# Scans of two prepared units moved behind later steps, and 21 products that nothing reads, in a fused RWKV-7 and hard-swish kernel

## The chip, the core and the metric

The kernel runs on one core of one Trainium2 chip. The metric is device time in microseconds (us) of one execution; the time of a version is the median of its runs. The core has a matrix engine (TensorE, PE in the profile, with the loads of its stationary operand shown apart as PEld), a vector engine (VectorE, DVE), a scalar engine (ScalarE, ACT), a general engine (GpSimd, POOL), and a queue that issues DMA transfers (SyncE, SP). Each takes its own instructions in program order; semaphores hold an instruction until what it needs is done.

## What is computed

The first half is the RWKV-7 recurrence over 4 batches, 8 heads, 768 steps and head size 40. The second is a feed-forward layer with hard-swish over the 3072 tokens, of width 320, with 2048 hidden features:

```python
for t in range(S):
    y[:, :, t] = einsum('bhd,bhde->bhe', rt, state)
    Sa = einsum('bhde,bhe->bhd', state, at)
    state = state * wt[:, :, None, :] - einsum('bhd,bhe->bhde', Sa, bt) \
            + einsum('bhd,bhe->bhde', vt, kt)
...
x = y.transpose(0, 2, 1, 3).reshape(B * S, H * D)
h = x @ w_in
out = (h * clip(h + 3.0, 0.0, 6.0) / 6.0) @ w_out
```

The two weight matrices arrive as 64-bit floats, which the kernel converts itself.

## The kernel before, in words

**Units.** Time is cut into blocks of 64 steps. A unit is one block of two of the four batches (128 rows) with all 8 heads; there are 24 units, and four consecutive ones (two blocks of both pairs of batches) make a group. Units 0 to 3 are the first group. For each unit the recurrence inside a block becomes dense algebra. `prepare` (line 532 on) makes what does not depend on the state: `W` turns the decays on PE (line 484) and multiplies them up with scans on DVE (lines 545, 549, 555); `gam` scans back and writes the decay factors (lines 564, 566, 568 and 579 on DVE, 583, 584 and 586 on POOL); then `A`, `B`, `K`, `F`, `E`, `EV` and `factor`. `step` (line 832) is the part that goes from unit to unit: `RT` and `VT` turn two inputs, `R`, `U` and `UT` solve for the block's updates with the inverse `tinv`, `C` and `H` are masked score products (line 522, masked on DVE at line 530), `sn` adds to the state (lines 961 and 969), `S` copies the turned state (lines 890 and 895), `rS` and `y` make the output, and `move` and `move2` bring it by 8 DMAs into the layout `xt` that the feed-forward part reads. A digit before a step is its unit: `2C` is the score product of unit 2.

**The inverse.** Each group needs the inverse of a triangular matrix for each head. `invert` (line 728) does the 32x32 parts on DVE in 30 dependent rounds of a product and a sum (lines 753 and 759) and ends with two transposes (lines 762 and 767). For the first group `third_block` then does the remaining blocks on PE, in two halves called `X` and `Y`: products at line 788, copied by ACT to `zs` (line 796), products at line 811, copied by ACT to `tinv` (line 821). The loop at line 1251 issues the rounds of the first inversion one instruction at a time; a counter `n` counts them, and at chosen values it slips in other work.

**Weights.** `load_weights` and `power` bring 20 pieces of the weights: a DMA (line 334), three ACT instructions (lines 384 to 386), and three DVE instructions (lines 369, 372, 360).

**Feed-forward.** `expand` (line 1060) makes hidden features on PE (line 1066), ACT and DVE apply the activation (lines 1081 and 1082, result `gt`), and `contract` (line 1099) multiplies by the second matrix (line 1107). `pieces` deals it out in small portions among the recurrence's work, so that PE always has something to do.

**Order around the change.** Nothing is scheduled automatically: the order in which Python issues is the order on each engine. Between the end of the first inversion and the steady loop the order is the table `PLAN` (line 1282), a row at a time. `P` and `Q` stand for units 4 and 5: the first mention runs the unit's `W`, the second its `gam`. `W` of unit 4 also issues two DMAs on SP that refill its input for unit 6. From row 8 on, counted from 0, feed-forward portions are dealt between the rows. The PSUM banks are shared: `one`, `o`, and buffers of two banks called `pair` and (until row 8) `lent`.

Of the kernel before, what the change touches and what calls it, by code (L numbers as in the profile page):

```python
# [17 lines left out]
P = 128  # L18
# [7 lines left out]
def _ap(ap, extra, dims):  # L26

    return bass.AP(tensor=ap.tensor, offset=ap.offset + extra, ap=[list(ap.ap[0])] + dims)
# [3 lines left out]
def kernel(  # L32
# [42 lines left out]
    nc = tc.nc  # L75
# [21 lines left out]
    def bank(tag, shape, bufs):  # L97
        return ps.tile(shape, F32, name=tag, tag=tag, bufs=bufs)
# [42 lines left out]
    def ps_pair(*dims):  # L141

        n = 1
        for d in dims:
            n *= d
        if shared[0] is None or shared[1] + n > 512:
            shared[:] = pair(), 0
            open_half[0] = None
        at = shared[1]
        shared[1] += n  # L150
        views, step = [], n
        for d in dims:
            step //= d
            views.append([step, d])
        t = shared[0][:]
        return [_ap(t, at, views), _ap(t, at + 512, views), _ap(t, at, [[512, 2]] + views)]
# [4 lines left out]
    ident = const.tile([P, P], F32, name="ident")  # L161
    nc.gpsimd.affine_select(
        out=ident[:], in_=ones, pattern=[[1, P]],
# [4 lines left out]
        out=ones[:, 0:BL], in_=ones[:, 0:BL], pattern=[[1, BL]],  # L168
# [3 lines left out]
        out=ones[BL:P, 0:BL], in_=ones[BL:P, BL:P], pattern=[[1, BL]],  # L172
# [7 lines left out]
    warm = const.tile([P, 1], F32, name="warm")  # L180
# [27 lines left out]
    start = const.tile([P, SCAN], F32, name="start")  # L208
# [167 lines left out]
    def power():  # L376

        to, raw = loaded[powered[0]]
        powered[0] += 1
        top = raw.rearrange("p n c t -> p n (c t)").bitcast(I16)[:, :, 3::4]  # L380
        if len(to.shape) == 4:
            top = top.rearrange("p n (j c) -> p n j c", c=to.shape[3])
        bits = to.bitcast(I32)
        nc.scalar.activation(out=bits, in_=top, func=AF.Identity, bias=low[:, 2:3], scale=1.0 / 16.0)
        nc.scalar.activation(out=to, in_=bits, func=AF.Prelu, bias=low[:, 0:1], scale=-1.0, alpha=2.0 ** -40)
        nc.scalar.activation(out=bits, in_=to, func=AF.Prelu, bias=low[:, 1:2], scale=-2.0 ** 63,
                             alpha=2.0 ** -40)
# [340 lines left out]
    def invert(F, third, alone=False):  # L728
# [46 lines left out]
            nc.gpsimd.tensor_copy(tinv[z + L:z + BL, :, L:BL], tb[z + L:z + BL])  # L775
        yield

    def third_block(F, tb, tt, n, zs, first=False):


        parts = [slice(0, H)]
        zp = ps_pair(H, L)
        for h in range(H):
            for y in range(2):
                for x in range(2):
                    z = x * BL
                    g = n * H + 2 * h + y
                    nc.tensor.matmul(out=zp[x][z + y * L:z + y * L + L, h, :], lhsT=F[z + L:z + BL, g, L:BL],
                                     rhs=tb[z + L:z + BL, g, :], start=True, stop=True,
                                     tile_position=(z + L, z + y * L))  # L790
        yield PE
        for part in parts:
            for x in range(2):
                z = x * BL
                for y in range(2):
                    nc.scalar.activation(out=zs[z:z + L, y, part], in_=zp[x][z + y * L:z + y * L + L, part],
                                         func=AF.Copy)
        if first:
            for part in parts:
                heads = slice(n * H + 2 * part.start, n * H + 2 * part.stop)  # L800
                for z in range(0, P, BL):
                    nc.gpsimd.tensor_copy(tinv[z:z + L, heads, 0:L], tb[z:z + L, heads])
                    nc.gpsimd.tensor_copy(tinv[z + L:z + BL, heads, L:BL], tb[z + L:z + BL, heads])
        shared[0] = None
        yield DONE
        tp = ps_pair(H, L)
        for h in range(H):
            for y in range(2):
                for x in range(2):
                    z = x * BL  # L810
                    nc.tensor.matmul(out=tp[x][z + y * L:z + y * L + L, h, :],  # L811
                                     lhsT=tt[z:z + L, n * H + 2 * h + y, :],
                                     rhs=zs[z:z + L, y, h, :], start=True, stop=True,
                                     tile_position=(z, z + y * L))
        yield PE
        for part in parts:
            for x in range(2):
                z = x * BL
                for y in range(2):
                    heads = slice(n * H + 2 * part.start + y, n * H + 2 * part.stop + y - 1, 2)  # L820
                    nc.scalar.activation(out=tinv[z:z + L, heads, L:BL],  # L821
                                         in_=tp[x][z + y * L:z + y * L + L, part], func=AF.Copy)
        shared[0] = None
        yield DONE


    def third_blocks(first=False):

        zs = inv.tile([P, 2, 2, H, L], F32, name="zs", tag="x", bufs=1)
        return [third_block(*third[-1], 2 * n, zs[:, n], first) for n in range(2)]  # L830
# [318 lines left out]
    def aside(n, weight=0):  # L1149

        for _ in range(n):
            if side and next(side[0], side) is side:
                side.popleft()
            due[0] += weight
            while due[0] >= 1:
                due[0] -= 1
                next(weights, None)
# [6 lines left out]
    def run(stage, steps=0, mixed=0, deals=0):  # L1164

        for at in stage:
            if at == DONE:
                return
            aside(steps, mixed)
            deal(deals)  # L1170
# [79 lines left out]
    n, cleared = 0, []  # L1250
    while not third:
        aside(1)
        if not third:
            n += 1
            if n in POWERS and powered[0] < len(loaded):
                power()
            if n in STEPS:
                next(weights, None)
            if converted[0] >= 2 and not cleared:
                cleared.append(True)  # L1260
                for z in range(0, P, BL):
                    nc.scalar.activation(out=tinv[z + L:z + BL, :, 0:L], func=AF.Copy, scale=0.0,
                                         in_=_ap(three[z + L:z + BL], 0, [[0, NH], [0, L]]))
            if n % EARLY == 0 and early:
                run(early.popleft())
# [6 lines left out]
    def block(i, j):  # L1272

        if i % NU < 2:
            if j == 0:
# [4 lines left out]


    PLAN = """X X:2 0U:4 0UT:2 1R
              0sn:2 0H:1 Y:2 P
              1U 1UT:2 0y P
              2RT:1 Y:1 Q
              1sn:1 1H:1 2VT:2 0move 0move2
              1y:2 2R Q
              2S:3 3RT:2
              1move 1move2 2U:2 2UT:1 2C:3
              3R:2 3VT  # L1290
              2rS:1 2sn:2 2H:2 3S:2
              2y:2 3U:1 3UT:1 3C:4
              3rS:1 3sn:2 3H:4 2move
              3y:3 2move2
# [193 lines left out]
```

## Time and profile before

| what | us |
|---|---|
| runs of the kernel | 790.04, 790.25 (median), 790.51 |
| the profiled execution: its own time | 791.42 |
| the profiled execution: its span | 789.70 |
| PE busy in the span | 729.7 |
| DVE busy | 496.0 |
| ACT busy | 320.6 |
| POOL busy | 174.7 |

The span reaches from the first to the last instruction of one profiled execution; 1.72 us lie around it. PE is busy for 92% of the span, but this is an average. From 300 to 500 us it is busy for 198.36 of 200 us; from 40 to 60 us for 4.87 of 20. All times in the text are from the span's start. PEclk is the share of the full TensorE clock that was granted: at 0.50 a product takes about twice as long.

### The profile page before, as it was taken

How to read it: one execution, taken by the hardware profiler on the slowest of the kernel's cores; microseconds unless marked ns; L12 is line 12 of the kernel's file. 1: busy time of each engine (PE TensorE's matmuls, PEld its weight loads, DVE VectorE, ACT ScalarE, POOL GpSimd, SP SyncE). 2: the span in 40 equal slices, each digit the busy share in tenths (PEclk: the TensorE clock that was granted, in tenths of full speed). 3: DMA queues.
4: the chain of work that ended last, by engine and by line, in shares of the span. 5: the costliest groups of instructions: out<-in, count | busy, mean ns of one | idle time of the engine just before them, and what ended most of it. 6: DMA issues, size and time to landing. Idle time of an engine off the chain costs nothing.

```text
span 789.7 us, 35306 instructions
## 1 busy us (share of the span) xinstructions
PE 729.7 (92%) x15832; PEld 619.4 (78%) x15832; DVE 496.0 (63%) x971; ACT 320.6 (41%) x664; POOL 174.7 (22%) x318
## 2 busy tenths in 40 slices
PE   5726888999999989999999999999999999999998
PEld 4625777778778778888888888888888888888886
DVE  7899867699545699345988445987435982323210
ACT  2376865324445334444334444335434225412211
POOL 6403111322232304112404212304312202000000
PEclk9865699999999999999999999999999999999999
DMA  9684453311333313223213223213221101110000
GB/s 122 114 201 123 109 165 70 70 27 36 56 62 60 64 28 57 50 44 67 44 29 64 45 46 63 48 28 65 45 51 38 31 10 30 30 30 10 13 20 17
DMA packets 174215, 45.03 MB, mean 57 GB/s; under 512 B 157424, under 2 KB 172784, under 8 KB 174064
## 3 DMA queue, kind: packets, MB, share of 16 engines
q1 hardware_dynamic: 169760, 42.03, 27.5%
q8 instruction: 125, 2.05, 1.0%
q10 hardware_dynamic: 4304, 0.74, 0.7%
q14 instruction: 26, 0.21, 0.1%
HBM read 34.08 MB, written 3.93 MB: 48 GB/s over the span
## 4 chain that ended last, share of the span: by engine, by line
PE 80%; DVE 8%; DMA 4%; issue 3%; ACT 2%; SPq 2%; POOL 0%; DVEq 0%
PE h L1066 27%; PE o L1107 24%; PE pair L522 4%; PE pair L984 3%; PE one L484 2%; PE pair L494 2%; PE pair L961 2%; PE pair L906 2%; PE pair L868 1%; PE pair L926 1%; PE pair L942 1%; SPq L468 1%; PE pair L811 1%; PE pair L701 1%; DVE wm L566 1%
## 5 line engine op out<-in xcount | busy, mean ns | idle before, releaser
L1066 PE MATMUL h<-xt,win 128*128 128x128 f32 (+1 forms) x2304 | 249.0, 282 | 3.3 <-DVE gt L1082 3.3
L1066 PEld LDWEIGHTS h<-xt,win 128*128 128x128 f32 (+1 forms) x2304 | 229.6, 191 | 20.3 <-issue 4.2
L1107 PE MATMUL o<-wout,gt 128*128 128x320 f32 x768 | 229.6, 442 | 0.0
L1107 PEld LDWEIGHTS o<-wout,gt 128*128 128x128 f32 x768 | 138.1, 190 | 50.2
L1082 DVE SCALAR_TENSOR_TENSOR gt<-gt,h 128x512 f32<-128x512 f32 x96 | 62.0, 681 | 74.4 <-ACT gt L1081 74.4
L1081 ACT ACTIVATE gt<-h,three 128x512 f32<-128x512 f32 x96 | 62.1, 686 | 96.0 <-PE h L1066 95.6
L996 POOL TENSOR_TENSOR yg<-ys,gam 128x512 f32<-128x512 f32 x22 | 39.0, 1772 | 156.7 <-DVE ys L995 77.1
L753 DVE TENSOR_TENSOR prod<-x 128x30 f32<-128x30 f32 (+9 forms) x180 | 67.2, 373 | 8.9 <-POOL x L738 3.3
L674 POOL TENSOR_TENSOR KBt<-K,rgt 128x320 f32<-128x320 f32 x22 | 19.0, 865 | 217.8 <-ACT rgt L663 169.6
L759 DVE TENSOR_TENSOR x<-x,prod 128x30 f32<-128x30 f32 (+9 forms) x180 | 62.2, 346 | 5.5
L969 DVE TENSOR_TENSOR state<-pair,state 40x320 f32<-40x320 f32 (+1 forms) x43 | 21.0, 488 | 62.8 <-PE pair L961 36.5
L530 DVE COPY_PREDICATED score<-mask,pair 128x512 f32<-128x512 int32 x72 | 50.6, 722 | 1.5 <-PE pair L522 1.0
L995 DVE TENSOR_TENSOR ys<-pair,ys 128x512 f32<-128x512 f32 x22 | 15.2, 690 | 40.5 <-PE pair L701 21.5
L566 DVE TENSOR_TENSOR_SCAN wm<-wm,start 128x528 f32<-128x528 f32 x24 | 37.7, 1571 | 0.8
L555 DVE TENSOR_TENSOR_SCAN prods<-wm,start 128x528 f32<-128x528 f32 x24 | 30.0, 1252 | 9.2 <-ACT wm L551 9.1
L846 ACT ACTIVATE RT<-pair 128x512 f32<-128x512 f32 x22 | 13.1, 597 | 54.2 <-PE pair L494 52.5
L706 ACT ACTIVATE EV<-pair 64x320 f32<-64x320 f32 x44 | 19.0, 432 | 33.1 <-PE pair L701 22.3
L821 ACT ACTIVATE tinv<-pair 32x256 f32<-32x256 f32 x48 | 18.0, 375 | 33.9 <-PE pair L811 33.3
L1125 ACT ACTIVATE ob<-o 128x320 f32<-128x320 f32 x22 | 9.6, 435 | 50.3 <-PE o L1107 26.0
L583 POOL COPY gam<-prods 128x256 f32<-128x256 f32 x24 | 22.0, 917 | 33.3 <-DVE prods L555 32.5
L984 PE MATMUL pair<-score,KBt 64*64 64x64 f32 x1408 | 26.1, 221 | 1.7 <-DVE score L530 1.4
L872 DVE TENSOR_TENSOR RR<-pair,EV 128x320 f32<-128x320 f32 x22 | 10.7, 486 | 26.0 <-PE pair L522 26.0
(272 smaller groups left out, 1078.4 us busy)
## 6 DMA issues: line engine op xcount, KB each, us to landing
V<-in_v_dram SPq DMA_DIRECT2D x96, 40.0 KB
out_dram<-ob SPq DMA_DIRECT2D x47, 80.0 KB
R<-in_r_dram SPq DMA_DIRECT2D x92, 40.0 KB
B<-in_b_dram SPq DMA_DIRECT2D x42, 80.0 KB
K<-in_k_dram SPq DMA_DIRECT2D x42, 80.0 KB
W<-in_w_dram SPq DMA_DIRECT2D x37, 80.0 KB
A<-in_a_dram SPq DMA_DIRECT2D x37, 80.0 KB
xt<-yg SPq DMA_DIRECT2D x72, 40.0 KB
```

What stands on the lines that cost most here:

```text
L522: nc.tensor.matmul(out=o[i][half(q), n, :], lhsT=lhs[half(i, D), n ^ (2 * q * swap), half(q)], rhs=rhs[half(i, D), n, half(q)], start=True ...
L530: nc.vector.copy_predicated(out=x[:].rearrange("p (i h) t -> p i h t", i=2), mask=mask8, data=o[2])
L555: nc.vector.tensor_tensor_scan(out=prods[:].rearrange("p r m i -> p (r m i)"), data0=wm[:, 0:SCAN], data1=start[:], initial=0.0, op0=ALU.m ...
L566: nc.vector.tensor_tensor_scan(out=back, data0=back, data1=start[:], initial=0.0, op0=ALU.mult, op1=ALU.add)
L753: nc.vector.tensor_tensor(out=pv, in0=_ap(x[:], (i + 1) * L + i, [[L, n], [0, i]]), in1=_ap(x[:], i * L, [[0, n], [1, i]]), op=ALU.mult,)
L759: nc.vector.tensor_tensor(out=rest, in0=rest, in1=pv, op=ALU.add)
L984: nc.tensor.matmul(out=y[q][half(s), pr, :], lhsT=o[name][half(q), h * D:h * D + SLOT], rhs=m[name][half(q), 4 * rs + 2 * s + j, :], start ...
L996: nc.gpsimd.tensor_tensor(out=yg[:], in0=m["ys"][:].rearrange("p r q t -> p r (q t)"), in1=o["G"][:], op=ALU.mult)
L1066: nc.tensor.matmul(out=hp[c][:, i, :], lhsT=lhsT, rhs=rhs, start=(begun[c] == 0), stop=(begun[c] == 3 * NQ - 1))
L1081: nc.scalar.activation(out=gt[:], in_=hp[c][:], func=AF.Relu, bias=three[:], scale=1.0)
L1082: nc.vector.scalar_tensor_tensor(out=gt[:], in0=gt[:], scalar=6.0, in1=hp[c][:], op0=ALU.min, op1=ALU.mult)
L1107: nc.tensor.matmul(out=op[:], lhsT=gts[c][:, n, :], rhs=wout[:, c * HJ + r * NQ + n, :], start=((split or r == 0) and c == 0 and n == 0), ...
```

## The change

Two edits. The first: in the loop of the first inversion, when the counter reaches 34, DVE sets a small tile to zero, and PE then runs one product that reads that tile and 15 products of the 128x128 identity with itself into the bank `o`. Nothing reads the results. Six more such products follow the first half's products of line 788. The second: in `PLAN` the entries `P` and `Q` (units 4 and 5, `W` and `gam`) leave rows 1 to 5 and stand in rows 7 to 9.

```diff
+    def unread(n):
+        o = bank("o", [P, 512], 1)
+        for _ in range(n):
+            nc.tensor.matmul(out=o[:, 0:P], lhsT=ident[:], rhs=ident[:], start=True, stop=True)
...
     def third_block(F, tb, tt, n, zs, first=False):
...
+        if first and n == 0:
+            unread(6)
         yield PE
...
             n += 1
+            if n == 34:
+                nc.vector.memset(warm[:], 0.0)
+                o = bank("o", [P, 512], 1)
+                nc.tensor.matmul(out=o[:, 0:1], lhsT=ident[:], rhs=warm[:], start=True, stop=True)
+                unread(15)
...
     PLAN = """X X:2 0U:4 0UT:2 1R
-              0sn:2 0H:1 Y:2 P
-              1U 1UT:2 0y P
-              2RT:1 Y:1 Q
+              0sn:2 0H:1 Y:2
+              1U 1UT:2 0y
+              2RT:1 Y:1
               1sn:1 1H:1 2VT:2 0move 0move2
-              1y:2 2R Q
+              1y:2 2R
               2S:3 3RT:2
-              1move 1move2 2U:2 2UT:1 2C:3
-              3R:2 3VT
-              2rS:1 2sn:2 2H:2 3S:2
+              1move 1move2 2U:2 2UT:1 2C:3 P
+              3R:2 3VT P Q
+              2rS:1 2sn:2 2H:2 3S:2 Q
```

On the engines this moves the following. PE: the four turns of the decays of unit 4 go from behind the second half's line 788 to behind `2C`, and those of unit 5 from behind the second half's line 811 to behind `3VT`, right before the first feed-forward product. DVE: of each unit two copies and a scan (`W`), and a reciprocal, a scan, a small fill and two scaled copies (`gam`); they go from before the multiplication of unit 0's and unit 1's output to between the mask of `2C` and the first `gt`. POOL: three copies of each unit, past the fill of `U` of unit 2 and the state scales of units 2 and 3. SP: the two refill DMAs for unit 6, from before the fetch of unit 3's `R` to behind the eight moves of unit 1, right before the weight pieces 15 to 19. Some `pair`, `lent`, `one` and `o` buffers change places.

## The prediction, made before the changed kernel ran

> **What bounds the kernel now.** I read the page's slices first, then the grants by stretches, then the timeline of 50 to 126 us. Slices are 19.7 us wide:
>
> ```profile
> PE   5726888999999989999999999999999999999998
> DVE  7899867699545699345988445987435982323210
> PEclk9865699999999999999999999999999999999999
> ```
>
> PE is full from the seventh slice on (198.36 of 200 us busy from 300 to 500), so whatever the start gains or loses before about 126 us stays to the end. The loss lies in slices 3 to 6, where PE is idle and its clock halved, and where DVE is near full. The stretches show when the grant moves (columns: stretch, length, busy time and instructions of PE, PEld, DVE, ACT, POOL, then the granted clock, DMA share, GB/s):
>
> ```profile
> 47.02:50.44 3.42, 3.33 (x16) 3.28 (x16) 3.25 (x8) 1.97 (x5) 0.00 (x0) 0.50 0.62 100
> 50.44:53.85 3.41, 1.54 (x66) 1.11 (x64) 3.21 (x9) 2.35 (x4) 0.00 (x0) 1.00 0.78 174
> 60.68:64.09 3.41, 0.96 (x64) 0.97 (x64) 3.34 (x5) 3.33 (x5) 0.93 (x2) 0.50 0.04 4
> ...
> 70.92:74.33 3.41, 3.35 (x130) 3.10 (x126) 2.99 (x6) 0.96 (x2) 0.26 (x1) 0.50 0.94 252
> ...
> 84.57:87.98 3.41, 3.41 (x96) 2.96 (x92) 3.38 (x6) 2.33 (x5) 0.88 (x2) 0.50 0.95 192
> 87.98:91.40 3.42, 3.42 (x100) 3.34 (x101) 3.28 (x7) 3.32 (x5) 1.74 (x5) 0.50 0.61 138
> 91.40:94.81 3.41, 2.57 (x102) 2.00 (x100) 3.18 (x9) 3.31 (x7) 0.00 (x0) 1.00 0.86 225
> 94.81:98.22 3.41, 1.14 (x37) 1.10 (x38) 3.24 (x7) 3.35 (x6) 0.00 (x0) 1.00 0.13 38
> 98.22:101.64 3.42, 3.42 (x19) 3.42 (x18) 3.32 (x7) 1.43 (x3) 0.00 (x0) 0.50 0.13 40
> ```
>
> The grant moves only on a grid 3.41 us apart. A stretch filled with 128x128 products (47.02) is followed by full clock, one busy for 1.54 us (50.44) by half. But 70.92 is as busy and stays at 0.50: its tiles are 64 or 32 wide. I count a 128-wide record whole, a 64-wide one at 0.6 to 0.95 (by how densely four fit), a 32-wide one at a quarter. So counted, 84.57 has 2.55 us and stays low, 87.98 has 2.8 and rises: the rise needs about 2.7. Falling: 1.84 us (26.54 to 29.96) fell, 1.76 us (108.46 to 111.87) of denser work held, so about 1.7.
>
> The timeline shows what the change touches, and which wait ends last (bracket: idle before, releaser):
>
> ```profile
> 63.13 1.08 PE L788 MATMUL lent<-tb,F 32*32 32x32 f32 x64 [9.56 <-DVE tb L762]
> 66.81 0.92 PEld L811 LDWEIGHTS pair<-zs,tt 32*32 32x32 f32 x58 [0.22 <-ACT zs L796]
> 67.91 1.56 ACT L821 ACTIVATE tinv<-pair 32x256 f32<-32x256 f32 x4 [1.15 <-PE pair L811]
> 75.06 1.11 PE L484 MATMUL one<-ident,W 128*128 128x128 f32 x4
> 83.00 1.11 PE L484 MATMUL o<-ident,V 128*128 128x128 f32 x4
> 91.05 0.48 DVE L872 TENSOR_TENSOR RR<-pair,EV 128x320 f32<-128x320 f32 x1
> 109.37 1.28 DVE L1082 SCALAR_TENSOR_TENSOR gt<-gt,h 128x512 f32<-128x512 f32 x2 [2.35 <-ACT gt L1081]
> 110.11 1.16 PE L1066 MATMUL h<-xt,win 128*128 128x128 f32 x8 [2.67 <-DVE gt L1082]
> ```
>
> PE's last long wait is at 110.11, for the first `gt`. There ACT set it: its queue of conversions is full from 103.34. I forecast when that `gt` comes.
>
> **The 15 and 6 products.** The fill stands behind the second 168-wide round, at 56.5 us, and costs that chain about 0.1 (a fill is 0.07). A float product makes two PE records (12 products of line 1066 before 102.57 are the 24 records shown), each 0.213 at half clock (four turns in 0.85) and 0.107 at full. So the burst needs at most 16 x 0.43 = 6.8 us, from 56.7 to 63.5; with the grant rising at 60.68 (3.4 us of burst lie before) it ends near 61.9. Its cover is PE's idle 9.56 us; without it, it would hold line 788 back by its length. The six end near 64.9, or 66.6 at half clock; line 811 waits for `zs` until 66.8, so they cost nothing. 60.68 to 64.09 then holds 1.24 + 0.1 + 0.44 = 1.8 us counted: held. 64.09 to 67.50 holds 0.84 of the six and a quarter of line 811: it falls at 67.50. The yield is line 811 at full clock: 1.10 us from 66.81 to ACT's start become 0.67, a gain of 0.43, with the fill 0.33.
>
> **The move, on PE.** Two sets of turns leave: 75.06 to 76.11 and 83.00 to 84.04, 2.09 us. The end of line 961 of unit 1, 85.99, becomes 83.6; the PE pause of 0.75 at 79.25 that ended with nothing ("issue") I keep. The stretch 81.16 to 84.57 now holds 0.9 (line 961) + 0.85 (line 522) + 0.85 (turns of V) + 0.15 = 2.75 instead of 2.3: by my count the clock rises at 84.57, not 91.40. Line 984 of unit 1, 87.86 before, starts at 85.4, and line 868 ends near 87.1.
>
> **On DVE.** The scans leave the stretch before `RR` of unit 2 and come back behind it. State update of unit 1 at 83.6 (86.96 before), conversion, mask, conversion, `yg`: 0.49 + 0.65 + 0.75 + 1.85 + 0.65 gives `RR` at 88.0 against 91.05; the next follows 0.4 later. From `RR`'s end slot to `gt` DVE has no gap, and its queue runs, with the start-to-start times of before: conversions, state scale and mask of `2C` 5.81 (93.44 to 99.25); unit 4's copies and scan 2.0 (85.00 on); 1.33; its second half 1.99 (91.45 to 93.44); unit 5's copies and scan 2.0; 1.48; state 0.41; 2.36; second half 1.99: 19.4 us. From 88.4 that is 107.8, against 109.37: a gain of 1.55. ACT is no longer last: `RT` of unit 3 near 91, `UT` at 94.7, the 24 records at 96.8 to 100.1, `ys` 101.3, two conversions and a copy, `gt` from 106.4.
>
> The moved turns of unit 5 sit in a `pair` buffer until DVE copies them at about 101; line 961 of unit 2 waits there 0.5 us, hidden since DVE adds the state only near 103. On SP the refill (1.67 us) comes before pieces 15 to 19, but SP reaches them near 103.4 instead of 105.45: its chain starts with `raw_x`, which waits for line 811 (83.07 before, 81.3 now). Unit 6's decays are read at 129. POOL's six copies wait for the scans; ahead of `U` of unit 3 stand only unit 4's, done by 101, 3 us before its turn. Without these covers each would cost its length.
>
> **Sum.** Whether the pause of 0.75 returns no row tells: between 0 and 0.75 more gain, I take 0.3, nearer to its staying since the instructions around it are the same. 1.55 + 0.3 = 1.85. The profiled execution's 791.42 becomes 789.57; it stood 1.17 over the median, so 790.25 becomes **788.4**.
>
> **Rivals.** *The clock holds.* Then PE is never late from line 811 to `RR`: DVE's queue from unit 0's state (73.03, now 72.6), run without a wait, comes to unit 1's at 78.4, `RR` at 82.8 and `gt` at 102.6, 6.8 us before 109.37, 783.5; if it falls half way, 787; I take 785.5. For it: after the burst no PE gap is over 1.5 us. Against it: the fall at 53.85, after a gap of 1.59. [...]
>
> *The move cancels.* 8.0 us of scans now lie on the way to `gt`; DVE's idle there was only 2.19 + 2.35. If `RR` came 1.55 us later than I have it, nothing would be left: 790.2. For it: DVE is 96% busy from 84 to 102. Against: the two sets of turns surely leave PE.
>
> *No clock at all.* If neither burst nor move raises the grant before 91.40, PE's 2.09 alone bring `RR` to 89.0 and `gt` to 108.8: 789.7.
>
> *Slower: DVE's run stretches.* One conversion of 0.42 took 1.51 at 113.64, beside POOL's product of 1.60. If POOL's copies of `gam`, two a unit, each stretch a neighbour by that 1.09, the run grows by 4.4 and `gt` comes at 112.2: 793.1. It decides from 1.55 on; from the same copies at 78.33 and 87.10 no DVE row was stretched by over 0.1, which speaks against it.
>
> **How the numbers follow.** Forecast 0.45; clock holds 0.21; cancels 0.13; no clock 0.07; slower 0.14. A measurement of this kernel tells about 0.2%, 1.58 us, from no change. The forecast's own range is 787.4 to 789.3; two thirds of it lie below 788.67. Faster 0.31 + 0.21 + 0.05 (a cancelled move with a shorter DVE run) = 0.57; same 0.14 + 0.07 + 0.07 = 0.28; slower 0.14 and a rest of 0.01, 0.15. The range 784.6 to 791.2 leaves out the clock held throughout and the stretched run's far end.
>
> **What would show it.** Full clock from near 60.7 to 67.5, half until near 84.6, full again; line 811 of the first half near 0.65 us; `RR` of unit 2 near 88 and the first `gt` of line 1082 near 107.6 with no wait for ACT before it; DVE without gaps between. PE from 126 us on unchanged, only earlier. Full clock through 70 to 84 would make me wrong to the fast side; `RR` after 89.5, or conversions over 0.6 us beside POOL, to the slow side. The grid's phase against the kernel is known from one execution only, and is the weakest link.

## The result: slower, and the profile after

The changed kernel took 797.03 us (median of 4 runs, 796.21 to 798.38) beside 790.38 for the kernel before (4 runs): ratio 1.0087, 95% interval 1.0072 to 1.0102. In a later session it was 796.50 (6 runs) against 792.20 (29 runs): 1.0063, interval 1.0045 to 1.0080. The forecast was 788.4, a gain; the kernel is slower by 4.3 to 6.7 us. The kernel before spreads more than its first three runs let one think: 788.59 to 799.10 over 130 runs in four later sessions, each on another chip. That is why each experiment below is set against runs of the kernel before of its own session.

The profiled execution took 797.34, its span is 795.6. In the code of the changed kernel lines shift: 788 is now 794, 811 is 819, 872 is 880, 984 is 992, 1066 is 1074, 1082 is 1090, 1107 is 1115; the unread products are line 782, the fill is 1264. An activation here is one instruction of line 1082 (1090 after the change), which writes `gt`, and a lull is a stretch in which PE mostly waits. The slices, as shown of before:

```profile
PE   4637788999999989899999999999999999999998
DVE  7898877689346699345798355888445982323210
PEclk9857889999999999999999999999999999999999
```

Slices 4 and 5 have the clock that was hoped for (slices 3 to 6: 5, 7, 8, 8 tenths against 6, 5, 6, 9). Little here tells of a loss; a tenth of a slice is 2 us. The stretches on this execution's own grid (columns as above: length; PE, PEld, DVE, ACT, POOL busy; granted clock; DMA share; GB/s):

```profile
56.38:59.79 3.41, 3.18 (x14) 3.12 (x15) 3.08 (x13) 2.99 (x5) 0.00 (x0) 0.50 1.05 345
59.79:63.20 3.41, 3.41 (x18) 3.41 (x18) 3.34 (x7) 3.32 (x5) 0.17 (x1) 0.50 0.45 95
63.20:66.62 3.42, 2.91 (x82) 2.44 (x81) 3.32 (x4) 3.31 (x6) 3.14 (x6) 1.00 0.02 5
...
80.27:83.69 3.42, 2.75 (x161) 2.40 (x161) 3.02 (x6) 2.71 (x6) 0.93 (x3) 1.00 0.30 91
83.69:87.10 3.41, 2.73 (x106) 2.45 (x106) 2.24 (x5) 3.29 (x6) 0.06 (x1) 1.00 0.53 115
...
104.16:107.58 3.42, 0.44 (x8) 0.24 (x6) 3.33 (x9) 3.39 (x6) 1.56 (x3) 1.00 0.90 277
107.58:110.99 3.41, 2.69 (x32) 2.47 (x36) 2.29 (x5) 1.68 (x3) 0.00 (x0) 0.50 0.98 316
110.99:114.40 3.41, 3.41 (x131) 3.26 (x128) 2.04 (x3) 0.53 (x2) 1.21 (x1) 0.50 1.02 238
```

Two things to see. The grid lies 0.9 us earlier against the work than in the profile of before (56.38 instead of 57.27, which is 60.68 less 3.41), so the 15 products ran at half clock until 63.20, nearly to their end. And the lull ahead of the first `gt` now falls into one stretch (0.44 us busy), after which the clock is halved for 6.8 us. The timeline, at the places shown of before:

```profile
57.17 6.48 PE L782 MATMUL o<-ident 128*128 128x128 f32 x30
63.58 0.75 PE L794 MATMUL lent<-tb,F 32*32 32x32 f32 x64
84.37 0.33 PE L522 MATMUL lent<-RT,UT 40*64 40x64 f32 x3 [1.35 <-issue]
87.83 0.48 DVE L880 TENSOR_TENSOR RR<-lent,EV 128x320 f32<-128x320 f32 x1
107.56 1.28 DVE L1090 SCALAR_TENSOR_TENSOR gt<-gt,h 128x512 f32<-128x512 f32 x2
108.30 2.08 PE L1074 MATMUL h<-xt,win 128*128 128x128 f32 x8 [3.70 <-DVE gt L1090]
110.30 1.99 PE L992 MATMUL pair<-score,KBt 64*64 64x64 f32 x64
```

`RR` of unit 2 comes at 87.83 (88.0 was forecast), the first `gt` at 107.56 (107.6 was forecast), with no wait for ACT. Up to here the forecast held in this execution: 1.81 us ahead of before. But PE's wait is 3.70 where it was 2.67, and what follows runs at half clock: 2.08 and 1.99 us, where before each took 1.16.

To follow the lag, number the 96 activations of line 1090 in DVE's order from 0 (start times, us):

| activation | before | after | lag |
|---|---|---|---|
| 0 | 109.37 | 107.56 | -1.81 |
| 2 | 119.06 | 119.55 | +0.49 |
| 4 | 138.73 | 139.96 | +1.23 |
| 12 | 192.88 | 193.78 | +0.90 |
| 14 | 211.86 | 216.39 | +4.53 |
| 26 | 313.17 | 317.37 | +4.20 |
| 95 | 778.37 | 784.28 | +5.91 |

The lead of 1.81 is gone by the third activation. Of the 7.7 us from -1.81 to +5.91, 3.0 are lost by activation 4, 3.6 between 193 and 212, where neither edit has an instruction, and 1.9 more between activations 26 and 28 (335.07 after, 329.01 before). For 193 to 212 the kernel before shows

```profile
190.08 0.66 PE L484 MATMUL one<-ident,W 128*128 128x128 f32 x4
...
192.59 0.75 PE L788 MATMUL pair<-tb,F 32*32 32x32 f32 x64
193.27 2.42 PE L1107 MATMUL o<-wout,gt 128*128 128x320 f32 x8
```

and the changed kernel

```profile
190.98 0.66 PE L484 MATMUL pair<-ident,W 128*128 128x128 f32 x4
...
195.41 0.75 PE L794 MATMUL pair<-tb,F 32*32 32x32 f32 x64 [1.87 <-ACT wm L551]
196.10 4.11 PE L1115 MATMUL o<-wout,gt 128*128 128x320 f32 x8
```

The turn of the decays sits in `one` before and in a `pair` buffer after. Line 794 needs a `pair` buffer next and waits 1.87 us until ACT has read the decays; the clock falls for one stretch (196.32 to 199.74), and eight products of line 1115 take 4.11 instead of 2.42. Where the 1.9 us near 330 come from is taken up with the blocks of PE's program below.

### The profile page after: what moved, and what is told of

Read it like the earlier page. It is cut to its first block, busy times and chain, and to the rows that moved or that the text cites. A ratio compares the mean times of both kernels' runs of the same rounds, so it can differ in the third digit from the quotient of the medians.

```text
span 795.6 us, 35398 instructions
## 1 busy us (share of the span) xinstructions
PE 735.4 (92%) x15876; PEld 624.7 (79%) x15876; DVE 496.2 (62%) x972; ACT 320.4 (40%) x664; POOL 175.4 (22%) x318
## 3 DMA queue, kind: packets, MB, share of 16 engines
q8 instruction: 125, 2.05, 1.1%
## 4 chain that ended last, share of the span: by engine, by line
PE 67%; issue 4%; DVE 3%; DMA 1%; POOL 1%; ACT 0%; SPq 0%; POOLq 0%
PE h L1074 23%; PE o L1115 22%; PE pair L522 3%; PE pair L992 3%; PE pair L494 2%; PE pair L969 2%; PE one L484 2%; PE pair L876 1%; PE pair L914 1%; PE pair L934 1%; PE pair L950 1%; PE one L898 1%; PE pair L701 1%; PE pair L634 1%; PE pair L794 1%
## 5 line engine op out<-in xcount | busy, mean ns | idle before, releaser
L759 DVE TENSOR_TENSOR x<-x,prod 128x30 f32<-128x30 f32 (+9 forms) x180 | 61.9, 344 | 5.8 <-DVE prod L753 0.5
L992 PE MATMUL pair<-score,KBt 64*64 64x64 f32 x1472 | 27.8, 225 | 1.4 <-DVE score L530 1.4
```

The source lines that it names most:

```text
L759: nc.vector.tensor_tensor(out=rest, in0=rest, in1=pv, op=ALU.add)
L992: nc.tensor.matmul(out=y[q][half(s), pr, :], lhsT=o[name][half(q), h * D:h * D + SLOT], rhs=m[name][half(q), 4 * rs + 2 * s + j, :], start ...
```

## The experiments

Each was compared with runs of the kernel before on the same chip in the same session. "First" is the start of activation 0, "12 to 14" the time between those two activations, both in the one profiled execution (before: 109.37 and 18.98).

| version | ratio to before, 95% interval | first | 12 to 14 |
|---|---|---|---|
| the change, again | 1.0063 (1.0045 to 1.0080) | 108.99 | 21.03 |
| the move alone | 1.0049 (1.0026 to 1.0072) | 108.80 | 22.34 |
| the products alone | 1.0017 (0.9987 to 1.0047) | 110.39 | 19.54 |
| ring stepped, in the kernel before | 1.0032 (1.0016 to 1.0048) | 109.19 | 22.42 |
| the change, ring put back | 1.0033 (1.0013 to 1.0053) | 109.59 | 20.37 |
| the same, last scan a row later | 1.0014 (0.9987 to 1.0040) | 107.23 | 18.99 |
| the move, ring put back | 1.0014 (0.9995 to 1.0034) | 111.25 | 19.02 |
| the same, last scan a row later ("mended") | 0.9994 (0.9975 to 1.0013) | 107.68 | 18.99 |
| mended, 12 products in the lull | 0.9986 (0.9971 to 1.0002), again 0.9977 (0.9958 to 0.9995) | 107.64, 107.79 | 19.47, 19.11 |

**The two edits apart.** The move alone keeps the products out; the products alone keep the plan of before.

> The move of the scans without the 21 products; the whole computation. Theory of the banks: unit 5's turn takes one more place in the two-place ring of banks from row 8 on, every later turn changes places, and at 191 us the decays of a later unit sit in a pair buffer that line 788's products wait for; that costs 3.5 us, and it comes with the move alone. Then this kernel has the same late wait of near 1.9 us at 195 and is 3 to 7 us slower than before: 793 to 797. Rival, the products do the harm (more PE work, a clock that falls afterwards): then this kernel is within 1 us of before, 789.5 to 791.

> The 21 products and the fill without the move; the whole computation. Theory of the banks: no bank changes places late, so no loss at 191; PE runs at full clock from near 61 to 70, which gives 0 to 1 us at the first gt: 789.0 to 790.5. Rival, the products do the harm: 44 more PE records shift every later fetch pause and the clock: 792 to 797.

Measured: 796.08 (10 runs) and 793.93 (10) against 792.66 (31). The move alone costs most of what the change costs; of the products alone no cost can be told. (The microseconds in the expectations were set for a kernel before at 790.4; beside these runs it stood at 792.66, so the ratios decide.)

**The ring of banks.** The banks for turns are taken from a ring, which at row 8 is reset to two places, `one` and a `pair` buffer. In the changed kernel the turn of unit 5's decays is taken after that reset, one place more, so every later turn of the kernel sits in the other place. Two runs tell this apart from the rest: one step of the ring in the changed kernel puts all later turns back, and the same step in the kernel before swaps them there and does nothing else.

```diff
     for t, line in enumerate(plan):
...
         limit[0] = {3: 15, 8: 17, 9: PIECES}.get(t, limit[0])
+        if t == 9:
+            ring.rotate(-1)
```

> Both edits, and one line that turns the ring of banks by one place after row 9, so that every later turn lands where it did before the change. Theory of the banks: the wait at 195 and the fall of the clock behind it are gone, 3.5 us of the 6.7 come back: 793.0 to 794.0; what stays is the loss between 104 and 118 us and a share of pauses. Rival, the banks are only where the loss shows: 796 to 798.

> The kernel before with one step of the two-place ring of PSUM banks at row 9 and nothing else, so that from there on each turn sits in the place in which the changed kernel has it. The theory of the banks: the turn of the decays near 191 us sits in a pair buffer, the product of line 788 that follows waits about 1.9 us for it, the clock falls, the stretch of 193 to 212 us takes 22.5 us instead of 19, and the kernel is 3.5 to 4.3 us slower than before. The theory that the scans beside the first activation cost the time (DVE's load): no change, within 0.5 us. The theory that the banks matter only where the rest is late too: 0.5 to 1.5 us.

> The changed kernel once more, beside the kernel before on this chip. If the loss is in the kernel itself (the swapped banks with the wait at 195 us, and PE's lull ahead of the first activation at half clock), it is again 5 to 7 us slower, the interval from state 12 to state 14 of the activation (193 to 216 us) is again near 22.5 us instead of 19. If most of the 6.7 us was the phase of that one session, the ratio is within 0.3% of one and the interval near 19 to 20.

Measured: put back, 794.73 (10 runs) against 792.66; stepped in the kernel before, 794.15 (12) against 792.20 (29); the change again, 796.50 (6) against 792.20. The kernel before, with nothing but the step, shows the changed kernel's wait line for line:

```profile
191.28 0.66 PE L484 MATMUL pair<-ident,W 128*128 128x128 f32 x4
...
195.71 0.89 PE L788 MATMUL pair<-tb,F 32*32 32x32 f32 x64 [1.86 <-ACT wm L551]
196.53 3.90 PE L1107 MATMUL o<-wout,gt 128*128 128x320 f32 x8
```

The wait for `wm` at this product stands in the traces of all four versions with swapped places (the change twice, the move alone, this one: 1.87, 1.24, 1.87, 1.86 us) and in no other trace. The same four, and no other, also stop twice before turns, 0.35 and 0.39 us near 133.5 and 136. So the ring costs: 0.32% added alone, 0.30% less when taken out of the change (1.0063 to 1.0033), and 0.35% less when taken out of the move alone (1.0049 to 1.0014, see the table), some 2.4 to 2.8 us. The first is a comparison within one session and its interval leaves out 1; the other two go across sessions. All are less than the 3.5 to 4.3 expected from one trace: the one execution's 3.4 (22.42 less 18.98) is not the mean over executions. The second profile of the change shows how it varies: the wait was 1.24, the clock held, the eight products kept their 2.42, and 12 to 14 took 21.03, between the 22.5 and the 19 to 20 that the expectation named.

**The last scan a row later.** The backward scan of unit 5 stands in row 9, between the state of unit 2 and the first activation. Moved one row on:

```diff
-              2rS:1 2sn:2 2H:2 3S:2 Q
-              2y:2 3U:1 3UT:1 3C:4
+              2rS:1 2sn:2 2H:2 3S:2
+              2y:2 3U:1 3UT:1 3C:4 Q
```

> As the one with the ring turned, and the second half of unit 5's scans moved from before the first gt to the end of row 10. Theory of the first gt: it comes near 106.6 instead of 107.6, PE waits 2.5 us for it instead of 3.7, and if the clock then holds at 107.7 the 2.3 us of half clock up to 114.5 are saved too: 790.0 to 792.0. Rival, the wait is ACT's and the clock falls anyway: 793 to 794, as without this edit.

> The move of the scans alone with the ring of banks put back and the second scan of unit 5 one row later; none of the products. What the prediction saw in the move (1.4 to 1.9 us earlier at the first activation) against what PE's longer lull gives back at half clock. If the whole lead is given back there, the time is within 0.7 us of before; if half of the lead stays, 0.7 to 1.5 us faster; if the scans cost more than they free, 1 us or more slower.

> The move of the scans just as in the changed kernel with the ring of banks put back, and nothing else: no products, and the second scan of unit 5 stays in row 9. The move as in the changed kernel stood at 1.0049 of before (1.0026 to 1.0072), and the ring alone, in the kernel before, at 1.0032. If the ring is all that the move costs, this is within 0.1% of before; if the scan in row 9 costs by itself, between the state of unit 2 and the second activation, it is 0.1 to 0.25% slower, where the version with that scan one row later stood at 0.9994.

Measured: with the products, 1.0014 where it was 1.0033; without them, 0.9994 where it was 1.0014. Both point to 0.2%, and in neither pair do the intervals part, so the worth of this step is likely and not shown. The first activation came at 107.23 instead of the 106.6 that was expected, PE waited 2.77 us for it, and the clock fell at 108.25 where it had been hoped to hold. The profile of the move alone with the ring put back, which keeps the scan in row 9, can't help: a stop of 2.31 us at 80.8 made its first activation late.

**The lull.** In the mended version the first activation is 1.69 us ahead of before, yet activation 2 only 0.29 (118.77 against 119.06). Its timeline, products of lines 1066 and 984 behind the lull at half clock:

```profile
108.42 1.53 PE L1066 MATMUL h<-xt,win 128*128 128x128 f32 x8 [2.89 <-DVE gt L1082]
109.88 1.99 PE L984 MATMUL pair<-score,KBt 64*64 64x64 f32 x64
```

Twelve products of the identity, which nothing reads, were put into that wait:

```diff
+            if t == 9:
+                pieces(2)
+                unread(12)
-            pieces(3 if t < BEGIN else 1.5 if t < BEGIN + 3 else 0)
+            pieces(1 if t == 9 else 3 if t < BEGIN else 1.5 if t < BEGIN + 3 else 0)
```

> The changed kernel with the ring of banks put back, the second scan of unit 5 one row later, and 12 more products that nothing reads between the second and the third portion of row 9, where PE waits 2.8 to 3.7 us for the first activation. If the fall of the clock there gives back the lead of the moved scans, the first activation stays near 107.3 us, the clock is full from there on, the third activation (index 2) comes at 116.5 to 117.5 us instead of 118.8, and the time is 1 to 2.5 us under the version without these 12 (793.95 where the kernel before was 792.66), about 0.1% faster than before. If DVE's queue and not PE sets the third activation, it stays at 118.5 to 119.5 and the time at that of before, and if the 12 products hold PE up, it comes after 119.5.

> The version before this one without the 1, 15 and 6 products near the end of the first inversion; the 12 at the first activation stay. Their worth by the prediction is 0.33 us plus what the clock does behind line 811. If they are worth no more, the time is within 1 us of the version with them; if they lengthen the chain by taking PE's queue at half clock, it is 0.5 to 1 us faster; if the lift of the clock reaches the state steps, it is 1 to 2 us slower.

> The version with 12 products in the lull at the first activation and none near the inversion once more, beside the one without the 12. It stood at 0.9986 of before with an interval from 0.9971 to 1.0002. If the 12 products save the fall of the clock, it is 1 to 2 us faster than the version without them and about 0.15% faster than before; if the lull is hidden anyway, the two are within 0.5 us.

Without the products near the inversion: 790.84 (12 runs) against 792.20, and 791.30 (12) against 792.74 (35). In both profiles the clock stays at 1.00 through the lull. In the second one the same work takes 1.16 each:

```profile
105.59 2.94 PE L782 MATMUL o<-ident 128*128 128x128 f32 x24
108.53 1.16 PE L1072 MATMUL h<-xt,win 128*128 128x128 f32 x8
109.62 1.16 PE L990 MATMUL pair<-score,KBt 64*64 64x64 f32 x64
```

Activation 2 comes at 117.85, 1.21 ahead of before, and activation 95 at 776.42, 1.95 ahead: a lead that is kept to the end. In the first profile PE came to the lull a microsecond later, and the twelve products ended at 109.5, after the activation of 107.64 that PE had waited for, so they held PE up:

```profile
106.60 2.94 PE L782 MATMUL o<-ident 128*128 128x128 f32 x24
109.38 1.06 PE L1072 MATMUL h<-xt,win 128*128 128x128 f32 x8
```

There activation 2 came at 118.57, 0.49 ahead, and activation 95 at 780.01, 1.64 behind. That the clock holds is seen in all six profiles with these products; all seven with the scans moved and without them lost it, so that much is shown. What the time gains by it is less sure. This is the fastest version, by 0.14% and 0.23%; only the second interval leaves out 1. Against mended, in the same session, it is 0.17% by the ratios (0.9977 to 0.9994), which their intervals don't part. With the products near the inversion as well it was 793.01 against 792.20, 1.0030 (1.0010 to 1.0050), slower than without them by 0.44%, more than the 0.5 to 1 us that the expectation allowed; the intervals don't meet.

**Products in idle time, and the blocks of PE's program.** The profile of that version has a stop that waits for nothing that the trace shows, in the middle of a row of products:

```profile
118.21 4.26 PE L1074 MATMUL h<-xt,win 128*128 128x128 f32 x29 [3.36 <-issue]
```

If PE's records, products and loads, are counted in order of time, most such stops in all traces stand at counts 256 apart (block 8 at record 2242, block 10 at 2754, block 18 at 4802, and so on). Those that don't are two in every version, before line 701 near 38 and 285 us, the pair at 133.5 and 136 named above, and one of 1.05 us in the kernel with the ring stepped. The page of the kernel before lists among its DMA queues (packets, MB, share):

```profile
q8 instruction: 125, 2.05, 1.0%
```

125 packets of 2.05 MB are 16.4 KB each, and 125 times 256 is 32,000, close to PE's 31,981 records. By these two counts a packet brings a block of 256 of PE's records, and the stops stand where one block ends and the next begins; such a place is called a limit here. The traces hold the time of each packet, and in them PE stopped where a packet was late: over the 18 profiles the 123 stops at limits end 1.0 to 1.9 us (median 1.42) after the packet before the limit has landed, and at the 2111 limits without a stop that packet had landed 1.2 us ahead or more (median 3.85). In the first profiles of before and of the changed kernel there are 8 such stops each, and they end 1.26 to 1.51 us after it. The packet for the stop above set out at 115.58, 4.6 us after the limit before it, where the median is 0.8; from 110 to 114 us the DMA engines were full (share 1.11), which may be why. Most limits pass without a stop: of some 124, 4 to 10 in a profile show one of some 0.25 us or more. But one such stop took 3.36 us. Four products are 16 records (a product and a load, each twice), so the 22 near the inversion push every later limit back by 88 records, into other instructions. Four runs tell their place from their work: the 21 full products cut to 32x32 by one column (same count, no work), or kept full with 42 small ones in PE's wait ahead of 47 us, which brings 88 to 256, so that the limits stand at their old instructions.

```diff
+    o = bank("o", [P, 512], 1)
+    for _ in range(42):
+        nc.tensor.matmul(out=o[0:32, 0:1], lhsT=ident[0:32, 0:32], rhs=ident[0:32, 0:1], start=True, stop=True)
     n, cleared = 0, []
     while not third:
```

With the plan of before:

> The products near the end of the first inversion alone (the plan of before), with the 15 and 6 cut from 128x128x128 to 32x32 by one column: as many instructions on PE at the same places, hardly any work for it. In all traces PE's stops marked issue stand at the same counts of PE records, 256 apart, and the page counts 125 instruction transfers of 16 KB. Theory of the instruction blocks: the products cost because they push each later block limit back by 88 records, into other work, so the small ones cost the same, 1 to 1.7 us over before (0.13 to 0.2%), with a stop of about 1.2 us at block 10 near 86 us. Rival, the work of the products (clock, PE's queue): the small ones cost nothing, within 0.5 us of before.

> The products near the end of the first inversion at full size alone (the plan of before), and 42 small products (32x32 by one column) before them, in PE's wait of 7.7 us ahead of 47 us: with the 88 records of the 22 that is one block of 256, so that from the inversion on the limits of the blocks stand at the same instructions as in the kernel before. Theory of the blocks: the cost is gone, within 0.6 us of before, and the stop near 86 us is gone with it. Rival, the work of the products: 1 to 1.7 us over before as with the products alone.

Measured: 0.9994 (0.9978 to 1.0009) and 1.0002 (0.9981 to 1.0023). There the expectation of the blocks failed: the small products cost nothing that can be told, and there was no stop at block 10. With that plan there is no cost to explain; the interval of the products alone, at 0.17%, takes in zero. With the mended plan and the 12 products in the lull:

> The mended version with both the products near the inversion and the 12 in the lull once more, as the measure for the next two. It was at 1.0030 of before (1.0010 to 1.0050), in two clusters of runs, 791.9 to 793.1 and 795.2 to 798.4, where the version without the products near the inversion was at 0.9977 to 0.9986 and its two profiles had no stop at block 15. If the cluster above is the stop of 3.35 us at the limit of block 15 near 118 us, there are again two clusters some 3 to 4 us apart; if the cost is the work of the products, one cluster at 1.002 to 1.004.

> That version with the 15 and 6 products near the inversion cut to 32x32 by one column, the 12 in the lull at full size. Theory of the blocks: limits stand where they stand in the version with full products, so the time is the same, 1.002 to 1.004 of before, some runs with the stop at block 15. Rival, the work of the products: the time of the version without them, 0.997 to 0.999.

> That version with the products near the inversion at full size and 42 small ones before them in PE's wait ahead of 47 us, so that the limits of the blocks stand at the same instructions as in the version without any (256 records later in count). Theory of the blocks: 0.997 to 0.999 of before, no stop near 118 us. Rival, the work of the products: 1.002 to 1.004.

Measured: full products 1.0020 (0.9996 to 1.0045), runs from 790.21 to 799.88, without two clear clusters; small ones 1.0017 (0.9998 to 1.0037); full ones with the limits put back 1.0000 (0.9983 to 1.0017). By the medians the small ones cost what the full ones cost, and putting the limits back takes most of it away, which speaks for the place and against the work; it is not shown, since the intervals of all three overlap and take in no change, and the 42 small products were not run without the others. The traces agree in part. The three with shifted limits stop at block 10 (1.71, 1.08 and 1.34 us, at 85.4 to 86.3, ahead of `RR` of unit 2) and at block 15 (3.36, 1.93 and 2.21, at 116 to 118); the two with the 12 products and no others have 0.41 and nothing over 0.25 at block 10, and nothing at 15. Put back, there is no stop at 118, but in its one profile

```profile
90.47 0.62 PE L992 MATMUL pair<-score,KBt 64*64 64x64 f32 x26 [2.33 <-issue]
```

at the instruction where the others had 0.41 and nothing: at one and the same limit the stop differs from execution to execution. Summed over the execution, its stops at limits come to 9.0 us, as many as the 9.1 of the first one with shifted limits; and the move alone, which adds no product, has 8.5. So where the limits lie is not the only thing that sets the sum. What fits these runs best is that a stop costs where PE is the one that others wait for; its size in the time stays open. Of the 1.9 us that the changed kernel lost near 330, 1.5 are of this kind: its profile has stops at limits of 0.82 at 326.36 and 1.23 at 332.85, the kernel before one of 0.53 at 327.46.

## Why the prediction was wrong, step by step

**What bounds the kernel: the step that failed.** "PE is full from the seventh slice on, so whatever the start gains or loses before about 126 us stays to the end", and, at the end, "PE from 126 us on unchanged, only earlier". That holds only if what PE runs and waits for behind the change stays the same. It did not: from row 8 on every turn changed places in the ring, and some 86 us after the last moved instruction this became a wait on PE and a stretch at half clock. The prediction knew that buffers change places and priced one of them, unit 5's turn, at 0.5 us hidden; it didn't follow the ring behind it, so the sum has no term for it. What the runs showed in its place is a cost of 0.30 to 0.35%, some 2.4 to 2.8 of the 4.3 us of the second session.

**The lull.** The wait for the first `gt` was read as the last long wait of PE, whose end the change brings forward. In fact its length mattered too. PE reached it earlier and waited longer (3.70 for 2.67), because DVE's queue had 19.4 us of work in front of `gt` whatever PE did. Before, the lull lay across two stretches of the grid, and the clock held:

```profile
105.05:108.46 3.41, 2.39 (x28) 2.08 (x26) 1.94 (x4) 3.31 (x6) 0.00 (x0) 1.00 0.44 127
108.46:111.87 3.41, 1.76 (x52) 1.64 (x56) 2.32 (x4) 3.35 (x6) 0.00 (x0) 1.00 1.09 363
```

Now it lay in one, with 0.44 us busy. The lead of 1.81 was given back within 12 us. The prediction had an estimate for this, a fall below about 1.7 us busy, from two stretches of before (after 1.84 us the clock fell, after 1.76 it held), and didn't apply it at 108. The length is not all: the kernel before with the ring stepped has the old lull, 2.68 us, in another phase of the grid, and there the clock fell too:

```profile
107.39:110.81 3.42, 0.88 (x7) 0.88 (x8) 1.62 (x3) 3.39 (x6) 0.00 (x0) 1.00 1.09 373
```

With the plan of before the clock fell here in this one of five profiles, with the scans moved and nothing in the lull in seven of seven.

**DVE, ACT, POOL.** `RR` at 88.0 and `gt` at 107.6 were forecast, 87.83 and 107.56 came, with DVE running without a gap and ACT no longer last; 108.99 in the second profile of the change. (The row at 83.00 that the prediction counts among the turns that leave is unit 5's, though it reads `V`: DVE copies its result to `wm` at 85.00.) The rival in which POOL's copies stretch DVE's conversions fell: the one long conversion, 1.50 at 113.56, is the one of before, and beside POOL's copies only one was stretched, to 0.63 at 96.56 from 0.42. That is just over the sign that the prediction set (0.6), but 0.2 us and not 4.4. This rival had the right side by a wrong mechanism.

**The products.** They ran from 57.17 to 63.65, at half clock until 63.20, instead of to 61.9: the grid's phase, which the prediction called its weakest link. So they held line 794 back by some 0.5 us (its input was complete at 62.91, it began at 63.58). ACT's queue hid that, but ACT came to `zs` at 65.91 instead of 65.22, so the gain of 0.33 was not there: unit 0's state came at 73.26, where the kernel before had it at 73.03 and 72.6 had been reckoned. Line 819 of the first half took 0.70, close to the 0.65 forecast. What the prediction did not see is that 88 more records move the limits of the blocks, though the profile of before already has eight stops at such limits; "the PE pause of 0.75" that it kept became two, 1.47 and 1.35.

**The clock.** Full from 73.44 to 76.86 and from 80.27 to 93.92, where it was forecast from 84.57. That paid for the two pauses, so that `RR` came on time was luck: it came by other ways than those in the sum. The prediction's count of what raises the clock is the author's estimate: its figure of about 2.7 us comes from two stretches of before, and the weights that it gives to 64- and 32-wide records are shown by no run. For 128-wide work it fits: 56.38 to 59.79 held 2.62 us of it (and 0.56 us of two one-column records, left out of the count) and no rise followed, 46.14 to 49.55 held 2.76 and one did. For narrower tiles the count decided little, since its weight for 64-wide records was left between 0.6 and 0.95: two stretches of almost only such records, 70.03 with 3.31 us and 76.86 with 2.98, raised the clock in this profile, while 70.92 of before with 3.35 had not.

**What stays open.** Of the 0.63 to 0.87%, the ring is 0.30 to 0.35. For the rest the move with the ring put back has 0.14% (interval -0.05 to 0.34), and the products on top of it 0.19% (1.0033 less 1.0014), which late blocks may account for; neither is parted from nothing by its own comparison. How much of the rest is the clock in the lull, how much late blocks, no run here tells.

## What to carry to other kernels

When a step that takes a buffer from a ring is moved past the ring's reset, list which place every later user gets, to the end of the kernel: here a wait of 1.87 us turned up some 86 us behind the last moved instruction, and one step of the ring was a cheap test. Of a lead of 1.81 us ahead of the lull nothing was left two activations later where the clock was halved behind it, and of 1.58 us in another version 1.21 were left where it held; so count the busy time of the stretches around a lull after the change, for several phases of the grid. The 22 products that nothing reads moved every later limit of PE's blocks by 88 records, so the control for padding is padding of the same count without the work.

## What the runs showed of the hardware

The granted clock changed only on a grid 3.41 us apart in the profiles of before and of the changed kernel. The grid has another phase against the kernel from execution to execution: in two profiles of the changed kernel the stretch from 59.79 to 63.20 us shows 0.50 and 0.74. After the lull ahead of the first activation the clock was 0.50 from 107.58 in the changed kernel and from 110.81 with the ring stepped, and stayed at 1.00 in before's profile. One unchanged kernel ranged over 10.5 us (788.59 to 799.10 in 130 runs). PE's 31,981 records came with 125 packets of 16.4 KB, 256 records to a packet. Where a packet landed late PE stopped and went on 1.0 to 1.9 us after it had landed (123 stops in 18 profiles, median 1.42); such stops took 0.25 to 3.4 us each, in one execution 2.2 us together (mended) and in another 9.1 (full products near the inversion and in the lull). Products that nothing reads kept the clock at 1.00 through a lull in six profiles of six, and without them it fell to 0.50 in seven of seven with the scans moved.
